# Where the bookkeeping of six orderings and the folding of row sums stand in a one-core routed-attention and PReLU kernel

## The chip, the cores and the metric

One core of one Trainium2 chip runs the whole program. The metric is the device time of one execution in microseconds. Three runs of the kernel before gave 957.65, 957.71 and 958.09; the median, 957.71, is the time before. A profile was taken of one further execution.

## The reference, cut to what matters

```python
# routing attention: B, H, S, D = 4, 8, 768, 64; 16 centroids per head
q_assign = argmax(normalised q . normalised centroids)   # cluster of each query
k_assign = argmax(normalised k . normalised centroids)   # cluster of each key
mask = q_assign[:, :, :, None] == k_assign[:, :, None, :]
scores = where(mask, q @ k.T / 8, -1e9)
attn = softmax(scores)
attn_out = attn @ v
# feed-forward: x is (3072, 512), d_ff is 2048
x = attn_out.transpose(0, 2, 1, 3).reshape(B * S, H * D)
h = x @ w_in
g = maximum(h, 0) + alpha * minimum(h, 0)
out = g @ w_out
```

## The kernel before, in words

**Pairs, steps and slots.** Two heads of one batch make a *pair*, n = 0 to 15. A pair is worked off in three *steps*. For pairs 0 to 9 the work is cut into two halves of the queries, and each half takes three steps; pairs 10 to 15 (`NO` = 10) are taken whole, in three steps. The steps are numbered u = 0 to 77 (`NS` = 78). Up to u = 24 (`TOGETHER`) one loop runs; from there the loop at line 1460 runs, and it alone is changed. There, three steps make one *triple*. It begins at a *boundary*: scores of three chunks of keys for the new pair (TensorE, L765), then the weighted sum over v of the pair before (L901, or L934 for pairs taken whole), then the scores of the other three chunks. After the boundary come twelve *slots*: two in the first step of the triple, five in each of the other two. I count them 0 to 11. In a slot stand, in this order: pieces that are due (`tick`), the next entry of `todo` (VectorE's masks L806, sums L816 to L829, transpose L835 and row sums L843), scatters from the queue `sorting`, pieces of the feed-forward net (`feed`), and, in the second and third step, work put there by `prep_at` (in the first step it stands ahead of `todo`). The feed-forward pieces are `hidden` (L1027, evicted by ScalarE at L1033, sloped by VectorE at L1019) and `final` (L1045); they fill TensorE.

All of this is one order written by hand. [...]

**Pairs taken whole** are sorted by cluster first, so that only near chunks need scores. What I call an *ordering* of such a pair runs, with the names of the code:

- `load` (SyncE, eight DMAs, L127) at the step in `ORDERS`;
- `order_features`, two VectorE transposes of 128x768 (L564);
- `order_sims`, eight matmuls (L572) into the one-bank PSUM pool `ps_m`, and `order_counts`, which one tick later starts a chain of VectorE pieces: L402, L403, L404, L405, L408, L410 at one tick each, L581 and the scan L586 eight and nine ticks after the first;
- `order_begins` (matmuls L598, `ps_m` again) eleven ticks after the first, `order_ranks` (L606 to L608) and `order_rows` (L615 to L619) one and two ticks later, `order_clusters` (L636 to L642) two more;
- 24 scatters (`order_scatter`, GpSimd's indirect DMA, L663) and six stage loads (`order_stage`, three DMAs each, L652), which `order_rows` queues in `sorting`; one slot takes one scatter;
- `order_load`, much later (L674 to L692), which fetches the sorted rows.

**Sums.** `rows_sums` (L843) leaves each row's sum in pieces. `total` (L856) folds them with one fp32 matmul into a tile of `ps_m`. `invert` (L869) takes the reciprocal from there at the next boundary and spreads it (L876); `normalise` (L1003) or `normalise_near` (L940) uses it. Before the change, `total` is the entry of `todo` for slot 11.

**One bank for many.** The pool behind `misc()` has a single buffer, shown in the profile as mps. Its users take turns: `prep_sims` (L381), `prep_clusters` (L442), `order_sims` (L572), `order_begins` (L598), `total` (L856), the second side of `weigh_near` (L934), `to_rows` (L964). Each waits until the reader of the one before is done: L402, ScalarE's L446, L402, L607, L869, L940, ScalarE's L967.

The loop with its slots:

```python
            todo.popleft()()
            while sorting:
                scatters, piece = sorting.popleft()
                piece()
                if scatters:
                    break
            feed(max(pieces, 0))
```

Of the kernel before, what the change touches and what calls it, by code (L numbers as in the profile page):

```python
# [23 lines left out]
def kernel(  # L24
# [347 lines left out]
    NX = GT * NG  # L372
# [117 lines left out]
    sorting = deque()  # L490
# [71 lines left out]
    def order_features(n, w):  # L562
        us[n, w] = raw_qk.pop((n, w)).rearrange("p h j d -> p (h j d)")
        nc.vector.transpose(out=us[n, w], in_=us[n, w])  # L564
# [80 lines left out]
    def order_stage(n, i):  # L645
# [5 lines left out]
        for src, p0, d0 in ((q, 0, 0), (k, TS, 0), (v, TS, D)):  # L651
            nc.sync.dma_start(out=t[p0:p0 + TS, :, d0:d0 + D],  # L652
                              in_=src[b, head, rows].rearrange("(x p) d -> p x d", p=TS))

    def order_scatter(n, i, x):
        h, part = divmod(i, PARTS)
        m = NX // PARTS
        xx = part * m + x
        if x == 0:
            nc.gpsimd.tensor_copy(  # L660
                out=sorts["stage"][i % STAGES].bitcast(I32)[0:TS, :, D],
                in_=sorts["number"][0:TS, part * m:(part + 1) * m])
        nc.gpsimd.indirect_dma_start(  # L663
            out=scratch[n][1][h * NX + xx],
            out_offset=bass.IndirectOffsetOnAxis(ap=ranks[n][:, xx, h:h + 1], axis=0),
            in_=sorts["stage"][i % STAGES][:, x, :], in_offset=None,
            element_offset=h * 2 * S * P)

    def order_load(n):
        whole = scratch.pop(n)[0]  # L670
        found = sorts["order"].tile([P, 2, NJ, 1], I32, name="found")
        for h in range(2):
            r0 = 2 * h * S
            nc.sync.dma_start(out=found[:, h], in_=whole.bitcast(I32)[  # L674
                r0:r0 + S, D:D + 1].rearrange("(j p) d -> p j d", p=P))
        orders[n] = found
        for w in range(2):
            raw = inp.tile([P, 2, NJ, D], FP32, name="qk")
            for h in range(2):
                r0 = (2 * h + w) * S  # L680
                for x in range(D // Q):
                    r = h * D + x * Q
                    nc.sync.dma_start(
                        out=raw.rearrange("p h j d -> p (h j d)")[r:r + Q, :].rearrange(
                            "p (t i) -> p t i", i=Q),
                        in_=whole[r0:r0 + S, x * Q:(x + 1) * Q].rearrange(
                            "(t p) i -> p t i", p=Q))
            raw_qk[n, w] = raw
        vt = vpool.tile([P, 2, NJ, D], FP32, name="vt")
        for h in range(2):  # L690
            r0 = (2 * h + 1) * S
            nc.sync.dma_start(out=vt[:, h], in_=whole[r0:r0 + S, D:2 * D].rearrange(  # L692
                "(j p) d -> p j d", p=P))
        vts[n] = vt
# [632 lines left out]
    FREE = SLOTS * SB - 3  # L1327


    ORDERS = [26, 30, 34, 38, 41, 51]  # L1330
    prep_at, load_at = {}, {}
    for (n, half), u in start_of.items():
        def at(step, slot, piece):
            prep_at.setdefault((step, slot), []).append(piece)
        if half is None:
            t = ORDERS[n - NO]
            load_at.setdefault(t, []).append(lambda n=n: load(n))
            for i in range(2):
                at(t + 2, 2 + i, lambda n=n, i=i: order_features(n, i))
            at(t + 3, FIRST + 1, lambda n=n: order_sims(n))  # L1340
            load_at.setdefault(u - (3 if n == NO + 1 else 4), []).append(
                lambda n=n: order_load(n))
            at(u - 4, 0, lambda n=n: prep_clusters(n))
            for i in range(2):
                at(u - 1, i, lambda n=n, i=i: order_blocks(n, i))
                at(u - 1, FIRST + i, lambda n=n, i=i: order_queries(n, i))
            continue
        if half == 0:
            if n < NCH:
                if n > 1:  # L1350
                    load_at.setdefault(max(u - 7, 0), []).append(lambda n=n: load(n))
                if n > 0:
                    load_at.setdefault(max(u - 6, 0), []).append(lambda n=n: load_v(n))
            else:
                load_at.setdefault(u - 9, []).append(lambda n=n: load(n))
                load_at.setdefault(u - 7, []).append(lambda n=n: load_v(n))
            if n < NCH:
                for g in range(len(groups)):
                    at(u - 4, FIRST + g, lambda n=n, g=g: prep_features(n, g))
            else:  # L1360
                for w in range(2):
                    at(u - 7, FIRST + w, lambda n=n, w=w: prep_blocks(n, w))
            at(u - (3 if n < NCH else 5 if u - 6 < TOGETHER else 6), FIRST,
               lambda n=n: prep_sims(n))
            if n >= NCH:
                at(u - 4, FIRST if u - 4 < TOGETHER else 0, lambda n=n: prep_clusters(n))
        if n < NCH:

            if half == 1 or n == 0:
                at(u - (3 if half else 1), FIRST,  # L1370
                   lambda n=n, half=half: prep_queries(n, half, 0))
            continue
        for h in range(2):
            at(u - 1, FIRST + h, lambda n=n, half=half, h=h: prep_queries(n, half, h))
# [87 lines left out]
    for u in range(TOGETHER, NS + 1):  # L1462
        for piece in load_at.get(u, []):
            piece()
        if u < NS:
            n, half, s = steps[u]
        if s == 0 or u == NS:
            prior = steps[u - 1][:2]
            assert not unfinished[0]
            tick()  # L1470
            if u < NS:
                score(n, half, range(0, NJ // 2), alone=NJ // 2 - 1)
            tick()
            if prior[1] is None:
                invert(prior[0], 0, 1)
                weigh_near()
            else:
                invert(*prior)
                weigh(GROUP if u == TOGETHER else NJ)
            if u < NS:  # L1480
                for chunk in last(NJ // 2):
                    mask(chunk)
            if prior[1] is None:
                normalise_near(prior[0])
            else:
                normalise(*prior)
            if u in begun_at:
                feed_block(u)
                if u < NS:
                    whole = len(ffn) - kept(u)  # L1490
            if u == NS:
                break
            tick()
            score(n, half, range(NJ // 2, NJ), alone=NJ // 2)
            E = last(NJ)
            for c in range(NJ // 2, NJ):
                todo.append(lambda c=c, E=E: mask(E[c]))
            if half is None:
                of = {c: e for _, _, c, e in E}
                todo += [lambda n=n, E=of: add_near(n, 0, E),  # L1500
                         lambda n=n: (turn(n, 0), rows_sums(n, 0)),
                         lambda n=n, E=of: add_near(n, 1, E),
                         lambda n=n: (turn(n, 1), rows_sums(n, 1))]
                todo += [lambda: None] * 4 + [lambda n=n: total(n)]
            else:
                todo.append(lambda E=E: add_up(E[1], E[0]))
                for c in range(2, NJ):
                    todo.append(lambda c=c, E=E: add_up(E[c]))
                todo.append(lambda n=n, half=half: (turn(n, half), rows_sums(n, half)))
                todo += [lambda: None] * 2  # L1510
                todo.append(lambda n=n: total(n))
            slots = range(3, SLOTS)
        else:
            slots = range(SLOTS)
        if u == TOGETHER + 1:
            order_constants()
        for i in slots:
            tick()
            if s == 0:
                prepare(u, FIRST + i - 3)  # L1520
            at_slot = (u - block_start(u)) // SB * FREE + (s * SLOTS + i - 3)
            room = (block_end(u) - block_start(u)) // SB * FREE
            pieces = len(ffn) - kept(u) + -whole * (room - 1 - at_slot) // room
            todo.popleft()()
            while sorting:
                scatters, piece = sorting.popleft()
                piece()
                if scatters:
                    break
            feed(max(pieces, 0))  # L1530
            if (s, i) == (SB - 1, SLOTS - 1) and unfinished[0]:
                feed(1)
            if s > 0:
                prepare(u, i)
# [223 lines left out]
```

## Time and profile before

| what | value |
|---|---|
| median of three runs | 957.71 us |
| the profiled execution, its own time | 958.22 us |
| its span, first to last instruction | 956.3 us |
| TensorE matmul busy | 929.1 us (97%), 3995 matmuls |
| VectorE busy | 669.4 us (70%) |
| ScalarE busy | 251.5 us (26%) |
| GpSimd busy | 297.8 us (31%) |
| granted TensorE clock, mean | 0.997 |

The span lies 1.9 us under the profiled execution's time, and that time 0.5 us over the median. Busy shares are averages over the whole span; the loop concerned runs from the boundary of u = 24, whose first score starts at 196.6 us, to the boundary of u = 78 at about 760 us. The first scores of the boundaries start at these times, us from the span's start:

| u | 24 | 27 | 30 | 33 | 36 | 39 | 42 | 45 | 48 |
|---|---|---|---|---|---|---|---|---|---|
| us | 196.6 | 223.5 | 263.3 | 289.5 | 324.9 | 353.8 | 388.0 | 419.6 | 452.5 |

| u | 51 | 54 | 57 | 60 | 63 | 66 | 69 | 72 | 75 |
|---|---|---|---|---|---|---|---|---|---|
| us | 478.0 | 517.2 | 540.7 | 571.5 | 614.7 | 652.9 | 680.2 | 707.0 | 733.6 |

### The profile page before, as it was taken

The page shows a single profiled execution, that of the slowest core. Times are in us where ns is not written, and L with a number is a line of the kernel's source. Part 1 is how long each engine was busy: PE and PEld are TensorE (multiplying, and loading weights), DVE is VectorE, ACT ScalarE, POOL GpSimd, SP SyncE. Part 2 cuts the span into 40 slices and gives each one's busy share as a digit, 9 for nine tenths or more (in the row PEclk, how much of TensorE's full clock was granted, in tenths as well). Part 3 has the DMA queues.
Part 4 walks back from the last instruction along what each step waited for, and adds up shares of the span by engine and source line. Part 5 has one row for each costly group of instructions (what it writes and reads, how often), then busy time and mean ns, then how long its engine had stood idle before and what let it go on. Part 6 is the DMA issues. An engine that isn't in the chain of part 4 may idle for free.

```text
span 956.3 us, 11347 instructions
## 1 busy us (share of the span) xinstructions
PE 929.1 (97%) x3995; PEld 496.8 (52%) x3995; DVE 669.4 (70%) x1235; ACT 251.5 (26%) x462; POOL 297.8 (31%) x333
## 2 busy tenths in 40 slices
PE   8999999999999999989999999999999999999997
PEld 5534444445454454444544545545455454556886
DVE  5797698799588697788894975556888536598100
ACT  5664544323032121220222212222122110221000
POOL 1433222210006365423277774640055440000000
PEclk9999999999999999999999999999999999999998
DMA  7433666047004444432842236441041011000000
GB/s 293 140 112 108 143 124 135 17 89 164 1 0 110 121 121 85 83 64 66 138 97 61 57 83 117 96 85 34 23 88 33 21 34 52 1 0 1 23 23 25
DMA packets 209664, 73.35 MB, mean 77 GB/s; under 512 B 194288, under 2 KB 198080, under 8 KB 209600
## 3 DMA queue, kind: packets, MB, share of 16 engines
q1 hardware_dynamic: 201840, 60.35, 28.5%
q0 software_dynamic: 6912, 11.81, 3.7%
q8 instruction: 33, 0.54, 0.2%
q10 hardware_dynamic: 848, 0.39, 0.2%
q14 instruction: 31, 0.25, 0.1%
HBM read 49.89 MB, written 22.28 MB: 75 GB/s over the span
## 4 chain that ended last, share of the span: by engine, by line
PE 77%; DVE 12%; issue 8%; POOL 2%; ACT 1%; DMA 0%; DVEq 0%; POOLq 0%; ACTq 0%
PE fps L1045 23%; PE fps L1027 17%; PE vps L901 7%; PE sps L765 6%; PE sps L1261 4%; PE sps L1205 4%; PE fps L765 2%; PE vps L1261 2%; PE vps L1205 2%; DVE acc L816 1%; PE fps L1261 1%; PE fps L1205 1%; DVE gT L1019 1%; DVE more L806 1%; PE vps L934 1%
## 5 line engine op out<-in xcount | busy, mean ns | idle before, releaser
L1027 PE MATMUL fps<-xT,w_in_sb 128*128 128x384 f32 x768 | 259.2, 491 | 0.0
L1045 PE MATMUL fps<-w_out_sb,gT 128*128 128x512 f32 x576 | 255.7, 596 | 1.1 <-DVE gT L1019 1.1
L663 POOL DMA_INDIRECT scratch<-stage,off x144 | 155.0, 1076 | 222.7 <-DMA stage<-in_v_dram 95.6
L1027 PEld LDWEIGHTS fps<-xT,w_in_sb 128*128 128x128 f32 x768 | 142.4, 190 | 103.6 <-issue 3.9
L1045 PEld LDWEIGHTS fps<-w_out_sb,gT 128*128 128x128 f32 x576 | 107.0, 190 | 129.0 <-issue 119.6
L972 POOL DMA_INDIRECT back<-rows,found x72 | 74.3, 1032 | 113.4 <-ACT rows L967 94.0
L1033 ACT COPY gT<-fps 128x384 f32<-128x384 f32 x96 | 46.0, 479 | 230.3 <-PE fps L1027 230.3
L1019 DVE SCALAR_TENSOR_TENSOR gT<-gT,alpha 128x384 f32<-128x384 f32 x96 | 61.5, 649 | 49.7 <-ACT gT L1033 49.5
L765 PE MATMUL sps<-qkT 64*128 64x384 f32 (+1 forms) x480 | 89.2, 490 | 0.0
L806 DVE SCALAR_TENSOR_TENSOR more<-aq,key,more 128x384 f32<-128x384 bf16 (+1 forms) x120 | 65.0, 598 | 19.3 <-ACT more L786 15.7
L786 ACT ACTIVATE E<-sps 128x768 f32<-128x768 f32 (+1 forms) x78 | 58.3, 796 | 62.5 <-PE sps L774 38.4
L765 PEld LDWEIGHTS sps<-qkT 64*128 64x128 f32 x480 | 42.8, 186 | 41.4 <-issue 14.4
L806 DVE SCALAR_TENSOR_TENSOR E<-aq,key,E 128x384 f32<-128x384 bf16 (+1 forms) x96 | 51.6, 595 | 17.7 <-ACT E L786 15.4
L901 PE MATMUL vps<-E,vt 128*64 128x384 f32 x316 | 58.6, 495 | 1.5 <-DVE xT L1003 1.5
L271 POOL TENSOR_TENSOR w_in_sb<-w_in_sb,power 128x512 f32<-128x512 f32 x16 | 26.9, 1683 | 67.8 <-DVE w_in_sb L268 67.8
L816 DVE TENSOR_TENSOR acc<-acc,E 128x768 f32<-128x768 f32 x37 | 35.2, 952 | 14.7 <-ACT E L786 13.6
L786 ACT ACTIVATE more<-sps 128x768 f32<-128x768 f32 (+1 forms) x42 | 31.4, 783 | 40.6 <-PE sps L765 40.0
L271 POOL TENSOR_TENSOR w_out_sb<-w_out_sb,power 128x512 f32<-128x512 f32 x16 | 22.6, 1412 | 56.0 <-DVE w_out_sb L268 56.0
L1051 ACT COPY y<-fps 128x512 f32<-128x512 f32 x18 | 10.6, 586 | 105.7 <-PE fps L1045 105.7
L1053 DVE TENSOR_TENSOR y<-y,fps 128x512 f32<-128x512 f32 x24 | 16.4, 683 | 29.8 <-PE fps L1045 29.8
L901 PEld LDWEIGHTS vps<-E,vt 128*64 128x64 f32 x316 | 20.1, 136 | 29.3 <-issue 26.8
L765 PE MATMUL fps<-qkT 64*128 64x384 f32 x144 | 31.8, 509 | 0.0
(281 smaller groups left out, 1106.1 us busy)
## 6 DMA issues: line engine op xcount, KB each, us to landing
raw<-in_moe_w_in_dram SPq DMA_DIRECT2D x16, 512.0 KB, 5.8
raw<-in_moe_w_out_dram SPq DMA_DIRECT2D x16, 512.0 KB, 4.3
out_dram<-y SPq DMA_DIRECT2D x21, 256.0 KB, 2.1
qk<-in_q_dram SPq DMA_DIRECT2D x48, 96.0 KB, 4.0
qk<-in_k_dram SPq DMA_DIRECT2D x48, 96.0 KB, 3.7
qk<-scratch SPq DMA_DIRECT2D x48, 96.0 KB, 3.4
w_in_kept<-w_in_sb SPq DMA_DIRECT2D x8, 512.0 KB, 4.7
vt<-in_v_dram SPq DMA_DIRECT2D x10, 384.0 KB, 4.3
```

Source lines behind the costliest of these rows:

```text
L271: nc.gpsimd.tensor_tensor(out=dst, in0=dst, in1=power[0].bitcast(FP32), op=ALU.mult)
L663: nc.gpsimd.indirect_dma_start(out=scratch[n][1][h * NX + xx], out_offset=bass.IndirectOffsetOnAxis(ap=ranks[n][:, xx, h:h + 1], axis=0), ...
L765: nc.tensor.matmul(out=bank(ps, h, m), lhsT=qkT[r:r + D, S + c * P:S + (c + 1) * P], rhs=qkT[r:r + D, tokens], start=True, stop=not early_ ...
L786: nc.scalar.activation(out=E[:, :, 0:m], in_=ps[:, :, 0:m], func=AF.Exp, scale=SCALE)
L806: nc.vector.scalar_tensor_tensor(out=e, in0=of, scalar=keys[n][:, NJ + c, h:h + 1], in1=e, op0=ALU.is_equal, op1=ALU.mult)
L901: nc.tensor.matmul(out=po[r:r + D, 0:HS], lhsT=vts[n][:, h, c, :], rhs=e[:, h, :], start=(c == 0), stop=(c == NJ - 1))
L972: nc.gpsimd.indirect_dma_start(out=to[i], out_offset=bass.IndirectOffsetOnAxis(ap=place[:, h, j:j + 1], axis=0), in_=rows[j // HJ][:, j % ...
L1019: nc.vector.scalar_tensor_tensor(out=gs[f], in0=gs[f], scalar=alpha[:, f:f + 1], in1=gs[f], op0=ALU.mult, op1=ALU.max)
L1027: nc.tensor.matmul(out=ps[:, 0:HS], lhsT=w_in_sb[:, c, f * P:(f + 1) * P], rhs=xTs[b, half][:, c, :], start=(c == 0), stop=(c == NCH - 1))
L1045: nc.tensor.matmul(out=ps[:, 0:DM], lhsT=gs[f][:, i * P:(i + 1) * P], rhs=w_out_sb[:, f, :], start=on and f == f0, stop=off and f == f0 + ...
L1205: nc.tensor.matmul(out=bank[to], lhsT=w_in_form(m, x, cc), rhs=rhs[:, cc, :], start=start and cc == 0, stop=cc == KH - 1, skip_group_check ...
L1261: nc.tensor.matmul(out=bank[to], lhsT=g_form(m, x, t), rhs=w_out_form(n, x), start=start and x == 0, stop=x == NQ - 1, skip_group_check=no ...
```

## The change

`ORDERS` moves four loads: pair 11 from step 30 to 29, pair 12 from 34 to 35, pair 15 from 51 to 50 (the other three stay), so that each stands in the last step of a triple. The features come one step after the load, in slots 0 and 1 of the next triple, and the similarities two steps after it, in slot 4. Before, they stood two and three steps after it, in whatever slot that gave. `total` leaves slot 11 and stands behind the first scores of the next boundary. A slot in the first step of a triple takes two scatters, every other slot one: 14 in a triple where there were 12. Two assertions and a record `scattered` are added that leave no instruction in the program.

```diff
-    ORDERS = [26, 30, 34, 38, 41, 51]
+    ORDERS = [26, 29, 35, 38, 41, 50]
...
-                at(t + 2, 2 + i, lambda n=n, i=i: order_features(n, i))
-            at(t + 3, FIRST + 1, lambda n=n: order_sims(n))
+                at(t + 1, FIRST + i, lambda n=n, i=i: order_features(n, i))
+            at(t + 2, 2, lambda n=n: order_sims(n))
...
             if u < NS:
                 score(n, half, range(0, NJ // 2), alone=NJ // 2 - 1)
+            total(prior[0])
             tick()
             if prior[1] is None:
                 invert(prior[0], 0, 1)
...
-                todo += [lambda: None] * 4 + [lambda n=n: total(n)]
+                todo += [lambda: None] * 5
...
-                todo += [lambda: None] * 2
-                todo.append(lambda n=n: total(n))
+                todo += [lambda: None] * 3
...
             todo.popleft()()
-            while sorting:
+            room = 1 + (s == 0)
+            while sorting and room:
                 scatters, piece = sorting.popleft()
                 piece()
-                if scatters:
-                    break
+                room -= scatters
             feed(max(pieces, 0))
```

More of the change, by code (lines that the diff above doesn't have):

```diff
@@ L653, in order_stage @@
                               in_=src[b, head, rows].rearrange("(x p) d -> p x d", p=TS))
+    scattered = {}
     def order_scatter(n, i, x):
+        scattered.setdefault(n, []).append((i, x))
         h, part = divmod(i, PARTS)
@@ L669, in order_load @@
     def order_load(n):
+        assert len(scattered[n]) == 2 * NX
         whole = scratch.pop(n)[0]
@@ L1521 @@
             at_slot = (u - block_start(u)) // SB * FREE + (s * SLOTS + i - 3)
-            room = (block_end(u) - block_start(u)) // SB * FREE
-            pieces = len(ffn) - kept(u) + -whole * (room - 1 - at_slot) // room
+            places = (block_end(u) - block_start(u)) // SB * FREE
+            pieces = len(ffn) - kept(u) + -whole * (places - 1 - at_slot) // places
             todo.popleft()()
-            while sorting:
+            room = 1 + (s == 0)
+            while sorting and room:
                 scatters, piece = sorting.popleft()
                 piece()
-                if scatters:
-                    break
+                room -= scatters
             feed(max(pieces, 0))
```

## The prediction

> **What bounds the kernel now.** I read the page first: how busy each engine is, and the chain that ended last.
>
> ```profile
> PE 929.1 (97%) x3995; PEld 496.8 (52%) x3995; DVE 669.4 (70%) x1235; ACT 251.5 (26%) x462; POOL 297.8 (31%) x333
> PE 77%; DVE 12%; issue 8%; POOL 2%; ACT 1%; DMA 0%; DVEq 0%; POOLq 0%; ACTq 0%
> ```
>
> TensorE is busy for all but 27 of 956 us. The change takes no arithmetic away from it, so only those 27 us can move. Next, the view of who waited for whom, for TensorE alone (total us, times, longest):
>
> ```profile
> PE mps L856 <- ACT rows L967: 3.6, 5, 1.1
> PE mps L856 <- DVE simT L402: 2.7, 3, 1.3
> PE mps L442 <- DVE begins L607: 2.2, 2, 1.9
> PE mps L856 <- DVE part L843: 1.7, 2, 1.3
> ...
> PE mps L934 <- DVE inverses L869: 1.3, 1, 1.3
> ...
> PE mps L381 <- DVE qk L940: 1.0, 1, 1.0
> ```
>
> Ten waits of the fold (L856), 8.0 us, and two of the clusters (L442), 2.2 us, are for the one mps bank or for late row sums. Third, the timeline of TensorE around boundary 45 shows how two of them arise:
>
> ```profile
> 406.67 0.50 PE L598 MATMUL mps<-simT,row 128*128 128x1 f32 x4
> 409.06 0.26 PE L442 MATMUL mps<-cluster,spread 128*128 128x24 bf16 x4 [1.89 <-DVE begins L607]
> 409.17 5.41 PE L1027 MATMUL fps<-xT,w_in_sb 128*128 128x384 f32 x16
> 414.51 0.85 PE L572 MATMUL mps<-qk,cT 128*32 128x384 f32 x8
> 416.62 0.40 PE L856 MATMUL mps<-part,fold 128*128 128x24 f32 x2 [1.26 <-DVE simT L402]
> ```
>
> Two users of the bank follow each other within a slot. The second waits until VectorE, at work on other things, has read the first out; the matmuls behind it stand meanwhile.
>
> [...] the 16 matmuls of L1027 at 409.17 need nothing from L442, yet come after its 1.89 us. [...] Here the fold's gap of 0.61 to 1.06 us before ACT's L967 repeats at five boundaries, behind one bank. [...] SyncE fetches ahead: the load written at step 30 is issued at 223.3 us, 40 us before that step.
>
> **The change, part by part.**
>
> *The fold leaves slot 11.* Gaps in front of it, by boundary: 30: 0.73 (L402), 33: 1.33 (L843), 36: 0.35 (L843), 42: 0.73 (L402), 45: 1.26 (L402), 54: 1.06, 57: 0.64, 72: 0.62, 75: 0.61, 78: 0.62 (all L967). Sum 7.95. The new place is 2.2 us of scores later, plus the rest of slot 11; the bank's reader has finished by then: L967 and L402 take 0.48 and 0.58, and L402 now stands six slots away. I take 7.95 off. The fold's own 0.37 us is paid in either place.
>
> *Clusters against begins.* L598 moves from slot 7 to slot 1, so no cluster step (slot 7) follows it: 1.89 and 0.32, 2.21 off. Together **10.16 us** removed.
>
> *What VectorE pays.* The reciprocals (L869) now wait for the fold behind the scores: 0.46 us from the fold's start to the first reciprocal (509.93 to 510.39), and 1.01 from there to the first mask (454.21 to 455.22). At boundary 48 the first scores end at 455.26, so masks start at 456.7, not 455.22. Cover is there: VectorE idles 1.16 before the normalising (L1003) and 0.79 before the next masks at 460.68, so the slip of 1.5 is over by then. The same sum over 17 boundaries gives 28.7 us of later masks (0 at boundaries 33 and 51, where VectorE is late anyway, 1.0 to 2.8 elsewhere). The usual idle, 1.20 plus 0.79, covers nearly each one; TensorE needs those masks a triple later. I cost it at nothing; without that cover it is the third case below. For pairs taken whole, the second side of L934 needs the reciprocals read: it comes 0.4 + 1.7 us after the scores, they end after 0.46 + 0.6. Free. The gaps 1.30 (L934) and 1.04 (L381) at boundary 51 come from VectorE's queue and stay. At the end (u = 78) no scores cover the fold, but nothing behind it needs it sooner than at a boundary.
>
> *New waits, each with both ends.*
>
> (a) Boundary 33. In triple 30, ahead of the row sums, VectorE gets pair 11's features (2 x 0.88), pair 10's rows 1.28 and clusters 1.39, pair 11's L402 to L405, 2.16; it loses pair 10's L405 to L410, 1.35. Net 5.2. Row sums ended at 286.4; plus 5.2, plus 0.6 of boundary slip, minus 1.15 of idle at 283: 291.0. The first scores then end at 291.7 - 1.33 = 290.4. A wait of 0.6; from 0, if operations overlap, to 2.0. I take 0.5.
>
> (b) Pair 15's similarities (slot 4 of triple 51) come right behind `to_rows` of pair 10, whose bank ScalarE copies out one tick later. Like the fold's waits on L967: 0.6 to 1.2 if an eviction is ahead in ScalarE's queue, nothing if that slot's piece is a `final` without one (at 494.5 it is). I take 0.5.
>
> (c) Similarities in slot 4 hold the bank until L402; clusters want it in slot 7, in triples 27, 42 and 51. Triple 42 is tight: adding VectorE's pieces up from the boundary gives L402's end at 407.5 to 408.8, against 408.4 on TensorE (407.2 plus 0.37 for the moved fold and 0.86 for L572). 0 to 1.5; I take 0.3.
>
> (d) L598 in slot 1 waits for the scan, now on VectorE right after the normalising. At boundary 33: about 301 on both engines. 0 to 1.0; I take 0.3. Elsewhere 2 us are free.
>
> Sum 1.6; upper ends 5.7, lower 0.
>
> *Queues.* GpSimd: 24 scatters of 1.08 us per ordering, as before; 12 or 14 in a triple is an order, not a speed, since GpSimd runs ahead of the slots as data allows and is 31% busy. The `order_load` of pair 10 stands at step 44, its scatters end near step 36 instead of 38. SyncE: eight loads of 0.6 us. Pair 12's now stand behind pair 10's last stages. Groups of four scatters, 5.5 us, alternating with landing and reloading a stage, 6.8, put the last stage near 305 us, the load's landing at 314; features are due near 333. Pair 15's is tightest: its buffer comes free with L699 (475.75 and 476.64 plus 0.9); 4.8 of issue and 4 of landing give 486, features are due at 488. Free, with 2 us to spare; VectorE's next idle (4.49 before 510.39) would take up a little more. Pair 10's order load and pair 8's load wait for L572 (11.5 and 12.5 us of SyncE's waiting) and come sooner; nobody waited for them.
>
> Net: 10.16 - 1.6 = 8.6 off 958.22 is 949.6 for the profiled execution; off the median, 0.5 lower, **949.1 us**.
>
> **Rivals.**
>
> *The waits change their names.* VectorE's work per ordering, some 10 us, is only shifted. If the late row sums (1.68) stay late at the new place, the clusters' 2.21 come back as waits for L402 instead of L607, and (b) and (d) cost 1.2 and 1.0, then 10.16 - 1.68 - 2.21 - 2.2 = 4.1 is left: **953.6**. For it: VectorE is 88% busy from 388 to 419.6 and is never idle from 461 to 505. Against it: five of the ten fold waits are ScalarE's and cannot return.
>
> *VectorE held at the reciprocals, slower than before.* In order as it is, it stands in front of L869 at every boundary until the fold has run; masks, normalising, sums slip, the next fold is late, and xT for new feed-forward blocks too. The price is the share of those 28.7 us that reaches TensorE; from 8.6 us (30%) on, the change costs time. At a half: 949.1 + 14.4 = **963.5**. It decides where VectorE has no idle left between normalising and the next masks. Against it: the 1.20 before L1003 and 0.79 before the masks stand in nearly all triples, and the two without have no slip.
>
> **How the numbers follow.** Forecast 0.62 (946.5 to 952.3), names changed 0.20 (to 957), held reciprocals 0.12, and 0.06 for a gain beyond 10.2. With (a) to (d) at zero it is 947.5, at their upper ends 953.2; the range runs to 955.5 to take in most of the first rival. Faster or slower means by over 0.2%, 1.9 us, about what a measurement can tell: faster 0.85, same 0.05, slower 0.10.
>
> **What would show it.** Right: in TensorE's waits, L856 and L442 are all but gone, and VectorE shows a wait for mps L856 in front of L869 at most boundaries. (a): a wait of L856 for L843 at boundary 33 alone; (b) L572 for L967; (c) L442 for L402; (d) L598 for L586. Wrong: L1045 or L1027 waiting for L1019 or L1003, folds that wait for L843 at several boundaries, or VectorE waiting for DMA in front of L564.

## The result, and the profile after

| | before | after |
|---|---|---|
| median | 957.90 us (4 runs: the three above and one of 959.21) | 947.93 us (4 runs) |
| the profiled execution, its time | 958.22 | 948.21 |
| its span | 956.3 | 946.3 |

The ratio of after to before is 0.9893, 95% interval [0.9876, 0.9911]: 10 us less. From here on the lines of the changed kernel behind about line 660 have numbers that are three or four higher: L856 is now L860, L869 is L873, L1027 is L1031.

The first view is the page: the busy times, and the chain that ended last.

```profile
PE 928.6 (98%) x3995; PEld 497.9 (53%) x3995; DVE 669.3 (71%) x1235; ACT 251.4 (27%) x462; POOL 296.8 (31%) x333
PE 90%; DVE 8%; issue 1%; ACT 0%; DVEq 0%; POOL 0%; POOLq 0%; ACTq 0%
```

No engine has less to do. TensorE's time without a matmul, span less busy time, falls from 27.2 us to 17.7, and its share of the chain rises from 77% to 90%. Who waited for whom, TensorE, three lines that concern the loop changed:

```profile
PE mps L598 <- DVE simT L586: 1.3, 1, 1.3
PE mps L938 <- DVE inverses L873: 1.2, 1, 1.2
...
PE mps L381 <- DVE qk L944: 1.0, 1, 1.0
```

The fold (now L860) and the clusters (L442) are not in the list at all. One line is new: the begins (L598) wait for the scan (L586). The other two were there before, 1.3 and 1.0. VectorE's list has at its top what was to be expected of reciprocals behind the fold (4.5 us, once, before):

```profile
DVE inverses L873 <- PE mps L860: 57.1, 14, 13.2
```

57 us of VectorE standing in front of the reciprocals, and TensorE is faster. VectorE's timeline at boundary 48, with the idle time and its releaser in brackets, shows why:

```profile
448.30 0.48 DVE L873 RECIPROCAL inverses<-mps 64x12 f32<-64x12 f32 x2 [1.56 <-PE mps L860]
448.81 0.58 DVE L880 STREAM_TRANSPOSE rd<-inverses 128x384 f32<-128x384 f32 x1
449.31 1.90 DVE L810 SCALAR_TENSOR_TENSOR more<-aq,key,more 128x256 f32<-128x256 bf16 x4
451.12 1.14 DVE L810 SCALAR_TENSOR_TENSOR E<-aq,key,E 128x384 f32<-128x384 bf16 x2
452.33 0.56 DVE L1007 TENSOR_TENSOR xT<-vps,rd 128x384 f32<-128x384 f32 x1
453.68 1.15 DVE L810 SCALAR_TENSOR_TENSOR E<-aq,key,E 128x384 f32<-128x384 bf16 x2 [0.80 <-ACT E L787]
```

The wait before normalising (L1007), 1.16 before, is used up; the 0.80 before the next masks, 0.79 before, is still there. So VectorE is no longer late by then: that cover held. Over the whole program such waits of the masks (for L783, now L787) fall from eight (5.6 us) to four (2.7), so elsewhere more of the cover was used; but L598's is the only new wait of TensorE.

The new wait stands in triple 54; this is TensorE's timeline there:

```profile
516.48 1.46 PE L769 MATMUL sps<-qkT 64*128 64x384 f32 x8
519.20 0.58 PE L598 MATMUL mps<-simT,row 128*128 128x1 f32 x4 [1.26 <-DVE simT L586]
519.64 2.83 PE L1031 MATMUL fps<-xT,w_in_sb 128*128 128x384 f32 x8
```

Between the last scores and L598 there is nothing: slot 0 of this triple has no feed-forward piece. The scan stands on VectorE behind two normalisings (pair 11 is taken whole) and ends at 519.06. What it reads (L581) was written by 501.93, and VectorE then stood idle for 10.31 us ahead of the reciprocals at 512.24; the scan still came behind them, at 518.11, in the order written.

### The profile page after: what moved, and what is told of

Same layout as the page of the kernel before. It is cut to its first block, busy times and chain, and to the rows that moved or that the text cites. A ratio compares the mean times of both kernels' runs of the same rounds, so it can differ in the third digit from the quotient of the medians.

```text
span 946.3 us, 11352 instructions
## 1 busy us (share of the span) xinstructions
PE 928.6 (98%) x3995; PEld 497.9 (53%) x3995; DVE 669.3 (71%) x1235; ACT 251.4 (27%) x462; POOL 296.8 (31%) x333
## 4 chain that ended last, share of the span: by engine, by line
PE 90%; DVE 8%; issue 1%; ACT 0%; DVEq 0%; POOL 0%; POOLq 0%; ACTq 0%
PE fps L1049 26%; PE fps L1031 24%; PE vps L905 8%; PE sps L769 7%; PE sps L1265 4%; PE sps L1209 4%; PE fps L769 3%; PE vps L1265 2%; PE vps L1209 2%; PE fps L1265 1%; PE fps L1209 1%; PE vps L938 1%; PE sps L778 1%; PE mps L938 1%; PE mps L381 1%
## 5 line engine op out<-in xcount | busy, mean ns | idle before, releaser
L1031 PE MATMUL fps<-xT,w_in_sb 128*128 128x384 f32 x768 | 257.7, 490 | 0.0
L666 POOL DMA_INDIRECT scratch<-stage,off x144 | 160.6, 1116 | 173.3 <-DVE acc L820 63.6
L1031 PEld LDWEIGHTS fps<-xT,w_in_sb 128*128 128x128 f32 x768 | 142.8, 190 | 102.8 <-issue 3.9
L976 POOL DMA_INDIRECT back<-rows,found x72 | 72.0, 1001 | 150.9 <-ACT rows L971 131.1
L873 DVE RECIPROCAL inverses<-mps 64x12 f32<-64x12 f32 (+1 forms) x44 | 10.9, 248 | 57.5 <-PE mps L860 57.1
L271 POOL TENSOR_TENSOR w_in_sb<-w_in_sb,power 128x512 f32<-128x512 f32 x16 | 23.7, 1481 | 69.8 <-DVE w_in_sb L268 69.8
L905 PEld LDWEIGHTS vps<-E,vt 128*64 128x64 f32 x316 | 20.1, 136 | 27.2 <-issue 24.4
```

The source lines that it names most:

```text
L271: nc.gpsimd.tensor_tensor(out=dst, in0=dst, in1=power[0].bitcast(FP32), op=ALU.mult)
L666: nc.gpsimd.indirect_dma_start(out=scratch[n][1][h * NX + xx], out_offset=bass.IndirectOffsetOnAxis(ap=ranks[n][:, xx, h:h + 1], axis=0), ...
L905: nc.tensor.matmul(out=po[r:r + D, 0:HS], lhsT=vts[n][:, h, c, :], rhs=e[:, h, :], start=(c == 0), stop=(c == NJ - 1))
L976: nc.gpsimd.indirect_dma_start(out=to[i], out_offset=bass.IndirectOffsetOnAxis(ap=place[:, h, j:j + 1], axis=0), in_=rows[j // HJ][:, j % ...
L1031: nc.tensor.matmul(out=ps[:, 0:HS], lhsT=w_in_sb[:, c, f * P:(f + 1) * P], rhs=xTs[b, half][:, c, :], start=(c == 0), stop=(c == NCH - 1))
```

## The experiments

My theory: TensorE stood because two users of the one mps bank, or the row sums and the fold, came too close in the order; moved apart, the waits go, and what VectorE loses at the boundary is covered. Rivals: the lighter triples of VectorE make the gain (the orderings, not the fold); and reciprocals held behind the fold cost time.

The runs of the fold moved alone, the orderings moved alone, the fold ahead of the first scores, the fold behind the weighted sum, and the last kernel came on two chips on which every kernel, the one before too (990.84 and 1005.25 us median beside them), was longer. TensorE pauses there for up to 22.7 us where the other runs show no wait, and what causes these pauses stays open. So of those runs the waits and the stretches ahead of the first pause (297 to 308 us, and 360 where the fold is moved alone) are read, and not the times. A wait behind the first pause counts only where both runs of a kernel show it. What was expected of a second run of a kernel rests on the trace of the first, so it is no forecast of its own.

### One scatter in every slot

```diff
-            room = 1 + (s == 0)
+            room = 1
```

> The changed kernel with one scatter in every slot again, 12 in a triple instead of 14. GpSimd runs ahead of the slots and nothing that it feeds is near due, so no change from the changed kernel: 947.9. If the 14 scatters carry part of the gain (order loads or stage loads that came sooner): 949 or more.

Measured: 947.77 us, ratio to before 0.9883 [0.9868, 0.9898], the same as the changed kernel's. The 14 scatters carry nothing of the gain.

### The rows one slot sooner, in the kernel before

```diff
-        starts = (6, 9) if dense else (6, 12)
+        starts = (6, 9) if dense else (6, 11)
```

> The kernel before with one number changed: the second turn of rows (to_rows, L964) and its scatters stand one slot sooner, in slot 9 and not 10, so that ScalarE's copy (L967) is a slot away from the fold in slot 11. If the five waits of the fold for L967 are the turn-taking at the one bank, they go and nothing else moves: 957.9 - 3.6 = 954.3. If ScalarE is simply late, or the wait finds another reader of the bank: 957 or more.

Measured: 957.59 us beside 958.38, ratio 0.9992 [0.9983, 1.0]: at most 1.6 us. The first theory's number (954.3) is missed; the second's (957 or more) holds. The waits say why: three of the five for L967 are still there, and longer, and one wait has found another reader of the bank (L446).

```profile
PE mps L856 <- ACT rows L967: 2.8, 3, 0.9
...
PE mps L964 <- ACT every L446: 0.6, 1, 0.6
```

The two that are gone stood ahead of boundaries 54 and 75. TensorE's timeline ahead of boundary 54:

```profile
505.15 0.49 PE L964 MATMUL mps<-ident,qk 128*128 128x128 f32 x3
505.48 3.60 PE L1045 MATMUL fps<-w_out_sb,gT 128*128 128x512 f32 x8
508.91 0.32 PE L856 MATMUL mps<-parts,fold 128*128 128x48 f32 x2
```

One that stayed, ahead of boundary 72, first in the kernel before and then here:

```profile
702.90 0.49 PE L964 MATMUL mps<-ident,qk 128*128 128x128 f32 x3
704.01 0.42 PE L856 MATMUL mps<-parts,fold 128*128 128x48 f32 x2 [0.62 <-ACT rows L967]
```

```profile
699.34 0.25 PE L442 MATMUL mps<-cluster,spread 128*128 128x24 bf16 x4
700.21 0.55 PE L964 MATMUL mps<-ident,qk 128*128 128x128 f32 x3 [0.62 <-ACT every L446]
700.60 2.75 PE L1027 MATMUL fps<-xT,w_in_sb 128*128 128x384 f32 x8
704.29 0.42 PE L856 MATMUL mps<-parts,fold 128*128 128x48 f32 x2 [0.95 <-ACT rows L967]
```

In all five places eight matmuls now stand between L964 and the fold, where the kernel before had none. What they are decides. At 54 and 75 they are a `final` (L1045) that ScalarE does not evict in that slot: the copy L967 starts at 505.68, as soon as its rows are there, and the wait is gone. At 57, 72 and 78 they are a `hidden` (L1027). The copy is written one tick after L964, behind that piece's own eviction (L1033) on ScalarE, so it starts only when the piece is done (703.75, after L1033 at 703.38), and the fold waits 0.95 where it waited 0.62 to 0.64. And the clusters' bank (L446) met the rows one slot on. So 1.67 us of waits went, and 0.97 and 0.62 came. A slot is a place in the order, not a time; here it parted two users of the bank only by the work in it, and only where that work put nothing ahead of the reader (no wait behind the `final`, 0.95 behind the `hidden`). This is for the turn-taking at the bank, and against my count of its price per slot.

### The fold moved alone

```diff
+            total(prior[0])
             tick()
...
-                todo += [lambda: None] * 4 + [lambda n=n: total(n)]
+                todo += [lambda: None] * 5
```

(and the same for halves; all else as before.)

> The kernel before with one part of the change: the fold (total) stands behind the next first scores; loads, features, similarities and scatters stay where they were. If the gain comes from taking the fold out of the queue for the one bank and out of the way of late row sums, all ten of its waits (7.95 us) go and the two waits of the clusters for L607 (2.21) and the 0.73 at the first scores of boundary 48 stay: 957.9 - 8.0 = 949.9. If the gain comes from VectorE's lighter triples, that is from the orderings, little goes: 955 to 957. If the reciprocals held behind the fold cost time, it is above 951.

> The fold moved alone, again. Bank turns: its ten waits (7.95) go, the clusters' 2.21 and the 0.73 at boundary 48 stay: 949.9. If the orderings' places made the gain: 955 or more. If the held reciprocals cost: above 951.

Measured: 984.07 us beside 990.84 (ratio 0.9925 [0.9863, 0.9986]) and 996.85 beside 1005.25 (1.0033 [0.9976, 1.0091]); these times say little, as told above. The waits agree in both runs: none of the fold is left; the clusters keep theirs; the begins, which in the old places fall on boundaries 36 and 57, now find the fold in the bank. These are lines of the second run:

```profile
PE mps L442 <- DVE begins L607: 2.3, 2, 2.0
PE mps L598 <- DVE inverses L869: 1.3, 2, 0.7
```

From boundary 24 to boundary 39, ahead of any pause, it takes 155.16 us in both runs; the kernel before takes 157.22, the changed one 154.38. So the fold alone is worth 2.1 of the 2.8 there. By the waits listed it is 1.75: three of the fold's (2.41) off, a new one of 0.66 on; the other 0.3 is not traced. Over the whole loop, by waits, 7.95 off and 1.3 on; what that is in time these runs do not show.

### The orderings moved alone

The changed kernel with `total` back in slot 11 (the previous diff, reversed). What is moved here are three loads, those of pairs 11, 12 and 15 (not four, as the section on the change has it), and the features and similarities of all six orderings.

> The changed kernel with the fold back in slot 11: only loads, features, similarities and scatters are moved. The waits for L402 (2.72), for L607 (2.21) and the 0.73 at boundary 48 go, the five for L967 (3.6) stay. VectorE's row sums of triple 30 end at 289.4 in the changed kernel, where slot 11 would come near 285.3: a wait of about 4 instead of 1.33, and some 0.8 in triple 42; the begins of pair 15 keep their new 1.26. Sum about -1.2: 956.7. If the orderings' places make the gain, it is 952 or less.

> Orderings and scatters moved alone, the fold in slot 11, again. Waits for L402 (2.72), L607 (2.21) and the 0.73 at boundary 48 go, those for L967 stay; the late row sums grow from 1.68 to 3.4 (boundary 33) and 1.1 (boundary 45) and perhaps 2.0 (boundary 57), and the begins of pair 15 may or may not wait: 955.5 to 958.5, so about nothing gained. If the orderings' places make the gain by themselves: 952 or less.

Measured: 1016.42 beside 990.84 and 1030.11 beside 1005.25 (ratio 1.0361 [1.0045, 1.0678]); not read. In both runs, ahead of the pauses, TensorE's timeline in triple 30 is this:

```profile
277.70 8.01 PE L1031 MATMUL fps<-xT,w_in_sb 128*128 128x384 f32 x24
289.10 0.37 PE L860 MATMUL mps<-part,fold 128*128 128x24 f32 x2 [3.39 <-DVE part L847]
289.31 4.52 PE L1031 MATMUL fps<-xT,w_in_sb 128*128 128x384 f32 x8
```

The fold waits 3.39 us for row sums that VectorE, with two orderings' pieces ahead, has not made; 1.33 before. And the eight matmuls behind it take 4.52 us where eight took 2.8 elsewhere. The view by windows has the granted clock of these stretches. It is the third value from the end, ahead of the DMA share and the GB/s:

```profile
285.70:289.10 3.40, 0.01 (x2) 0.03 (x1) 3.37 (x7) 0.48 (x1) 2.79 (x3) 1.00 0.43 116
289.10:293.80 4.70, 4.70 (x12) 2.25 (x12) 3.64 (x9) 0.00 (x0) 3.51 (x6) 0.64 0.30 83
```

Behind these 3.4 us of idleness the granted clock was 0.64 on average over the next 4.7 us, and the eight matmuls took 1.7 us more. From boundary 24 to 33 this kernel takes 96.8 us, against 92.9 before, 91.5 changed and 90.5 with the fold alone. Moved alone, the orderings lose 3.9 us there: 2.06 of longer waiting for row sums, 1.7 at the lower clock, and 0.85 for the similarities of pair 11, which only moved in from the next triple, less the 0.73 that the fold waited at boundary 30 before. That rival falls, for this stretch. A second late fold, 1.0 to 1.1 us, stands at boundary 45 in both runs.

The waits of the two experiments, put together, say which part removes which:

- Five for L967 (3.6 us): the fold. They are gone in both runs with the fold alone; with the orderings alone the last three stand as before, 0.61 to 0.62, in both runs.
- Two for late row sums, L843 (1.68): the fold. With the orderings alone the one at boundary 33 grows to 3.39, the small one at 36 is not there, and one of about 1.1 comes at 45.
- Three for L402 (2.72): either part removes them, since either moves one of the two users of the bank.
- Two of the clusters (2.21): the orderings. With the fold alone they stay, 2.3 us in both runs.

The two parts need each other: the orderings crowd triples 30 and 42 for VectorE, and only the fold's later place makes that harmless; the fold alone runs into the begins.

### The fold ahead of the first scores

```diff
             tick()
+            total(prior[0])
             if u < NS:
                 score(n, half, range(0, NJ // 2), alone=NJ // 2 - 1)
-            total(prior[0])
```

> The changed kernel with the fold at the boundary too, but ahead of the first scores, so 2.2 us sooner. If masks that slip cost nothing, only two things move: the row sums of triple 30 (end 289.4, boundary 33 at 288.5) give a wait of 0.9, and the wait of the begins in triple 54 (1.26) goes, since VectorE has its reciprocals sooner: 947.6. If the reciprocals held behind the scores cost time at many boundaries, this gives it back: 945 or less.

Measured: 993.52 beside 990.84, not read (a pause of 13.5 us stands at 298). Ahead of it, at boundary 33, the expected wait is there, 0.82 for 0.9, in this one run:

```profile
289.16 0.37 PE L860 MATMUL mps<-part,fold 128*128 128x24 f32 x2 [0.82 <-DVE part L847]
```

With slot 11 (3.39), this place (0.82) and the changed one (none), three places of the same fold show the row sums of triple 30 passing through: TensorE reaches it at 285.7, 288.3 and 290.6 us, and the first 2.6 us later take 2.6 us off the wait. Whether the wait of triple 54 goes, as expected, and what the sooner place does at other boundaries, could not be read behind the pauses.

### The fold behind the weighted sum

```diff
             else:
-                invert(*prior)
                 weigh(GROUP if u == TOGETHER else NJ)
+                total(prior[0])
+                invert(*prior)
```

(`total` ahead of it stays for pairs taken whole; `invert` must follow it.)

> The changed kernel with the fold behind the weighted sum as well, at the twelve boundaries where the pair before is worked in halves: about 4 us later, so VectorE's reciprocals and masks slip by 6 us there instead of 2. The slip of 2 is covered by idle time, the next 4 are not. If what it costs is what is due next, then waits of the begins for the scan after boundaries 30 to 45 (0.7 to 1.7 each) and of the first feed-forward pieces for xT at boundaries 36 and 48 (2 to 2.6 each) come up, 7 to 10 us in all: about 956. If VectorE's lateness reaches TensorE as a share of all slips (30% or more of 48 us): 962 or more. If VectorE has room for all of it: 948.

> The fold behind the weighted sum at the twelve boundaries of pairs worked in halves, again. What is due next pays: the begins (L598) wait some 3.7 to 4.8 for the scan at boundaries 30, 39, 42 and 45, the first feed-forward piece some 0.7 for xT at boundary 36, and boundary 51 finds its row of transposes late by 2.5: 947.9 + 17 + 0.7 + 2.5 = 968 at most, 962 if the lateness at 51 is caught up. If VectorE's lateness were a common tax at all twelve boundaries, waits would stand at 48, 57, 60, 63 and 66 too: over 970. If VectorE has room: 948.

Measured: 1028.28 beside 990.84 (ratio 1.036 [1.0279, 1.044]) and 1045.43 beside 1005.25; not read as times. Both runs wait at the four boundaries named, and at the first, ahead of any pause, TensorE's and VectorE's timelines show how:

```profile
269.82 1.46 PE L769 MATMUL sps<-qkT 64*128 64x384 f32 x8
275.00 0.98 PE L598 MATMUL mps<-simT,row 128*128 128x1 f32 x4 [3.72 <-DVE simT L586]
```

```profile
269.18 0.47 DVE L873 RECIPROCAL inverses<-mps 64x12 f32<-64x12 f32 x2 [14.06 <-PE mps L860]
...
273.90 0.95 DVE L586 TENSOR_TENSOR_SCAN simT<-mine 128x384 f32<-128x384 bf16 x1
```

The waits of L598 are 3.72, 3.72, 4.42 and 4.76 in the first run, 3.71, 4.76, 4.34 and 5.18 in the second, plus the clock (0.50 granted from 275 to 279). The first run's expectation had these four places right and their size wrong (0.7 to 1.7 each). It also had xT waited for by 2 to 2.6 at boundaries 36 and 48: it is 0.6 at 36 in both runs, and nothing at 48. And it left out boundary 51, where the first scores wait 2.5 in both runs for VectorE's transposes (L703). At 48 and 66 no wait stands on L1007 or the row sums. So a held reciprocal is not a tax on every boundary; it costs where something of TensorE's hangs on VectorE soon after, here the begins behind the scan and the scores behind the transposes. The third case of the prediction has its mechanism, but 4 us further out than the change goes.

### The begins of pair 15 later, and the similarities of pair 9

```diff
-        later(len(pieces) + 3, lambda: order_begins(n))
+        later(len(pieces) + 3 + (n == NP - 1), lambda: order_begins(n))
```

> The changed kernel with the begins of pair 15 alone one slot later (slot 2 of triple 54, where a feed-forward piece stands between). Its wait of 1.26 us for the scan goes: 947.9 - 1.3 = 946.6. If VectorE is late there as such, the wait comes back behind it (L607 or the row sums) and the time stays at 947.9.

Measured: 948.33 us, ratio 0.9886 [0.9871, 0.9901]. The wait stayed, 1.26: slot 1 of triple 54 has no work for TensorE either. Again a slot that parts nothing. The next kernel has this and, for the similarities (`prep_sims`) of pair 9, one slot later:

```diff
-            at(u - (3 if n < NCH else 5 if u - 6 < TOGETHER else 6), FIRST,
+            at(u - (3 if n < NCH else 5 if u - 6 < TOGETHER else 6), FIRST + (n == NO - 1),
                lambda n=n: prep_sims(n))
```

> As the run before, and the similarities of pair 9 one slot later (slot 1 of triple 51), so that they no longer ask for the bank while VectorE still has the second side of pair 10 to normalise: another 1.04 us goes, 945.6. If VectorE's queue is what is late, the 1.04 comes back in front of a later user of the bank or in front of L1049: 946.6.

Measured: 947.65 us, ratio 0.9883 [0.9868, 0.9898]. Here the slot has a piece in it, and the 1.04 us is gone, with no new wait behind it; the 1.26 of the begins is still there:

```profile
478.64 1.24 PE L769 MATMUL sps<-qkT 64*128 64x384 f32 x8
479.82 2.85 PE L1031 MATMUL fps<-xT,w_in_sb 128*128 128x384 f32 x8
482.59 0.85 PE L381 MATMUL mps<-qkT,cT 128*32 128x384 f32 x8
```

One us of 948 is below what these runs tell apart in time; the profile shows it. Last, the begins five slots later (`+ 5 * (n == NP - 1)`), with the other edit kept:

> The changed kernel, the similarities of pair 9 one slot later and the begins of pair 15 five slots later (slot 6 of triple 54), with feed-forward pieces of TensorE surely between the scan and the begins. Both waits (1.26 and 1.04) go and nothing comes back: 947.9 - 2.3 = 945.6. If VectorE's queue is what is late, one of them comes back in front of the next user of the bank: 946.6 to 947.9.

Measured: 1021.45 beside 1005.25, ratio 1.0329 [1.0227, 1.0431], on the second of the two chips with pauses. Its profile has neither of the two waits, and the begins of pair 15, at 567.37, follow a feed-forward piece without a gap; but pauses stand ahead of them and behind.

Whether this version is faster than the changed kernel stays open.

## Why the prediction was right, point by point

- **The ten waits of the fold and two of the clusters, 10.16 us.** Right: neither line is left in the profile after. The fold moved alone has none of its ten, and the orderings moved alone have neither of the clusters' two.
- **VectorE's slip at nothing.** Right for what the change does: masks at boundary 48 start 1.4 us after the first scores (1.5 was worked out), and no wait for a mask or a sum stands behind it. The fold 4 us later shows where the cover ends.
- **(a) Boundary 33, taken at 0.5:** nothing. The term was mis-sized by both of its ends. Row sums end at 289.4, not 291.0. Of the 1.6 us between, 0.5 is pair 10's L581, which left this triple too and which the sum left out; another 0.5 is pair 11's L402 to L405, which took 1.70 for 2.16, since VectorE starts the next instruction before each has ended (L402 at 281.63 is 0.57 long, the next starts 0.50 later); the rest is the slip at the boundary, which began 0.5 sooner than before. The first scores end at 290.7 for 290.4: the similarities of pair 11 (0.85) had moved into this triple, and the sum left them out. The fold in slot 11 shows that the worry itself was sound.
- **(b), (c), taken at 0.5 and 0.3:** nothing, at their lower ends. L572 of pair 15 at 490.98, and L442 in triple 42, the tight one, at 405.28, follow the piece ahead of them without a gap.
- **(d) Begins behind the scan, taken at 0.3 at boundary 33, "elsewhere 2 us are free".** Right mechanism, wrong place and size: 1.26 at triple 54, none at 33. Where the slot ahead is empty nothing is free.
- **"The gaps 1.30 and 1.04 at boundary 51 stay":** 1.16 and 1.04. Right.
- **Missed:** 0.73 at boundary 48. Before, the third chunk of the first scores waited for a bank of fps that VectorE, late with pair 14's clusters, had still to read (L1053). The view of TensorE's waits does not list it; it shows as a long group, and in the weights:

```profile
453.72 1.54 PE L765 MATMUL fps<-qkT 64*128 64x384 f32 x4
```

```profile
454.35 0.29 PEld L765 LDWEIGHTS fps<-qkT 64*128 64x128 f32 x2 [0.45 <-DVE y L1053]
```

After, the same four take 0.81 us: pair 14's ordering, which stands sooner, has left that stretch. This part of the gain is the orderings': the four take 1.77 and 1.76 with the fold alone, 0.81 in both runs with the orderings alone.

The sum: 8.6 forecast, plus 1.3 for (a) to (c), minus 1.0 for (d), plus 0.73, plus 0.14 at boundary 51, plus 0.5 behind the last matmul (6.98 to 6.51, not traced further) is 10.2; the two spans, 956.35 and 946.29, differ by 10.1.

**The rivals.** "The waits change their names": one did, at L598; the five of L967 did not come back, as argued. "Reciprocals held": not at this distance.

## What to carry to other kernels

Where several users take turns at one bank, list for each pair of neighbours what the contended engine has to do between them; here a slot of the written order that held no work for it parted nothing (the begins one slot later still waited 1.26 us), and a piece whose eviction was queued ahead of the reader parted nothing either (the fold waited 0.95 us for 0.62). When an engine is made to wait with its list behind it, as VectorE was here for 10.31 us with the scan behind, ask what the contended engine takes from it next and how soon: it was free at boundary 48 with the fold 2 us later, and cost 3.7 to 5.2 us a time with the fold 4 us later still, where a small matmul hung on it. Two moves that each fill a gap can depend on each other: the orderings alone lost 3.9 us from boundary 24 to 33, in the crowded triple that the fold's later place made harmless.

## What the runs showed of the hardware that was not expected

A pause of TensorE had a second price in some places here, and its length alone did not say whether it had. Behind the wait of 3.39 us (fold in slot 11, two runs on two chips, at the same place) the granted clock was 0.64 over 4.7 us in the first run and 0.63 over 4.6 us in the second; in the first, eight matmuls of 2.8 us took 4.5. Behind the waits of 3.72 and 3.71 us (begins in the late-fold kernel, one in each run) it was 0.50 and 0.70 over 4 us. Behind the wait of 1.89 us ahead of 409 us in the kernel before it was 1.00 to 414.5 us, and 16 matmuls took 5.41. With the fold moved alone, a wait of the clusters of the same length came out both ways. These are TensorE's timelines of the first run and of the second:

```profile
411.00 0.26 PE L442 MATMUL mps<-cluster,spread 128*128 128x24 bf16 x4 [2.01 <-DVE begins L607]
411.12 5.41 PE L1027 MATMUL fps<-xT,w_in_sb 128*128 128x384 f32 x16
```

```profile
412.25 0.27 PE L442 MATMUL mps<-cluster,spread 128*128 128x24 bf16 x4 [2.00 <-DVE begins L607]
412.37 7.09 PE L1027 MATMUL fps<-xT,w_in_sb 128*128 128x384 f32 x16
```

The granted clock of the 4 us behind the wait is 1.00 in the first and 0.57 in the second, and the same 16 matmuls take 1.68 us more. Both stand behind the first pause of their runs, at 360 us.

So a wait of 2.00 us was once followed by 1.68 us more than its own length; what decides between the two is not shown. My prediction priced a wait at its length alone. In the profiles before and after that was enough, since the granted clock is 1.00 over the loop (196 to 760 us) in both.
